# Attention in front of two feed-forward blocks on one core: row sums in 32-column products, transposes two pairs ahead

## The chip, the core and the metric

The kernel runs on one core of a Trainium2 chip. Its metric is the device time of one execution in microseconds. A core has five engines with queues of their own, each strictly in the order of the program: TensorE (PE: matmuls and transposes, fp32 results into PSUM), VectorE (DVE), ScalarE (ACT), GpSimd (POOL) and SyncE (SP, here for DMA issues alone). They meet through semaphores only: an instruction whose input or whose buffer is not ready holds up all that stands behind it on its engine. PSUM has eight banks of 128 partitions by 512 fp32.

## The reference

```python
def _attn_ref(q, k, v, cap):                      # 2 batches, 12 heads, 448 rows, 64 wide
    scores = np.matmul(q, k.transpose(0, 1, 3, 2)) / np.sqrt(64)
    scores = cap * np.tanh(scores / cap)
    scores = scores - np.max(scores, axis=-1, keepdims=True)
    attn = np.exp(scores)
    attn = attn / (np.sum(attn, axis=-1, keepdims=True) + 1e-09)
    return np.matmul(attn, v)
```

The heads side by side are the input (896 tokens by 768) of a feed-forward block (768 to 2048 to 768, with h * sigmoid(1.702 h)), whose output goes through a second one (RMS norm, a gate and a value of 1536, a projection to 768). All is fp32; the result must have nearly fp32 accuracy.

## The kernel before

**Numbers in two parts.** Most products are made of a high part in the type float32r and a rest: hi*hi + hi*lo + lo*hi, one pass of the array each. A product of plain fp32 operands (P*V, the row sums, transposes with the identity) needs no parts; the trace shows two passes for such a product. Weights are taken apart on the fly, unit by unit: `square`, `sign`, `mask` (ScalarE), `mid`, `top`, `low` (VectorE), `high_part` (ScalarE), `low_part` (VectorE), each on 128 x 768, each needing the one before. The first four units are decoded during attention: the list `early` (line 399) has 30 such steps, 15 for each of the two engines, and `decode(n)` emits the next n at its place in the loop. `low(w)` also issues the load of unit w + 3.

**Attention, pair by pair.** Two heads make a pair p (0 to 11); they lie side by side on the 128 partitions. For a pair
- `load_kq` and `load_v` bring k, q and v for a group of one to three pairs (`GROUPS`) over SyncE's queue, in chunks of 128 rows and a last one of 64;
- `turn(p)` transposes k and q on TensorE, eight 128 x 128 transposes into PSUM pool `ps_t` (one buffer);
- `split_kq(p)` makes the high parts and rests `x` on VectorE (two operations on 896 columns), and GpSimd copies the last 64 rows of k into a block-diagonal tile `kb`;
- `scores(p, c)` makes a strip of 128 key rows for c = 0, 1, 2, below also S(p,c): six passes on half the array's rows, two side by side, into pool `ps_s` (two buffers). `scores_last(p)` makes the last 64 rows of both heads in one strip of three full passes, into `ps_v` (two buffers);
- `exps(p, c)` is two operations on ScalarE: tanh, which frees the PSUM buffer, below tanh(p,c), and exp into tile `tt` (six buffers) or `tl`;
- `outputs(p)` is P*V, below P*V(p): six fp32 products on 64 columns of the array (tile position by head), then one on all 128 columns for the last strip, into `ps_v`; VectorE copies it to `z`;
- `add_two` (VectorE) and `add_third` (GpSimd) add the three wide strips of exponentials into `ts`; `sums(p)` multiplies `ts` by ones on 64 columns and the last strip by `blk` on 128, into `ps_v`;
- of pairs 0 to 8 the sums go by a short way: VectorE copies them to `sc`, GpSimd's DMAs fold one row of each head over 64 partitions (`rs`), `recips` (three iterations later) takes 7 reciprocals a partition and writes them to DRAM (`recs`), `spread` brings them back as a broadcast over 128 partitions (`r`, below r(p)). Pairs 9 to 11 take a reciprocal of 128 x 448 out of PSUM;
- `normal(p)` multiplies and takes the result apart into `xA` (VectorE: `norm_mul`, `norm_hi`, `norm_lo`; the copy of pairs 10 and 11 on ScalarE).

**The order.** Nothing is scheduled by a planner: the loop at line 420 emits the work of iteration p, and each engine executes its share in that order. A buffer is handed on in the order of allocation: with two buffers, the n-th tile of a pool waits for the last reader of tile n - 2. Iteration p is: S(p,1), exponentials of strips 0 and 1, `turn(p+1)`, `split_kq(p+1)`, `recips(p-3)`, `add_third(p-1)`, `spread(p-3)`, P*V(p-1), a decode step, S(p,2), S(p+1,0), the last strip, their exponentials, `normal(p-4)`, `add_two(p)`, two decode steps, `sums(p-1)`, loads. Iteration 12 holds what is left of pair 11, whose norm is emitted in the next stage.

**The next stage** (`rest`) runs the feed-forward blocks in one stream of matmuls (lines 521 to 523 and 724). It begins with three column blocks on the first 384 tokens (`HEAD`, 54 matmuls), then the same on the other 512, which need all twelve pairs.

Of the kernel before, what the change touches and what calls it, by code (L numbers as in the profile page):

```python
# [18 lines left out]
def attn_moe_kernel(  # L19
# [156 lines left out]
    def attention():  # L176
        with ExitStack() as actx:
# [12 lines left out]
            raws = [{nm: ap_.tile([128, NC + 1, 6 - 2 * i, D], F32, name=f"{nm}{i}", bufs=1) for nm in "kq"} for i in range(2)]  # L190


            vns = [ap_.tile([128, NC, 6 - 2 * i, D], F32, name=f"vn{i}", bufs=1) for i in range(2)]
            ves = [ap_.tile([128, 3 - i, 2, D], F32, name=f"ve{i}", bufs=1) for i in range(2)]
            kbs = [ap_.tile([128, 2, 128], F32R, name=f"kb{i}", bufs=1) for i in range(2)]

            def constants():
                for r in raws:
                    for nm in "kq":
                        nc.gpsimd.memset(r[nm][64:128, NC], 0.0)  # L200
# [9 lines left out]
            xs, pt, zt, nr, ts_ = {}, {}, {}, {}, {}  # L210

            def rows(src_, p0, n, c):

                b, h0 = divmod(2 * p0, H)
                return src_[b, h0:h0 + 2 * n, c * 128:min(c * 128 + 128, S)]

            def load_kq(g, nm, src_, eng=None):
                t, (p0, n) = raws[g % 2][nm], GROUPS[g]
                for c in (*range(NC), NC):
                    m = 128 if c < NC else 64  # L220
                    (eng or nc.sync).dma_start(out=t[0:m, c, 0:2 * n], in_=rows(src_, p0, n, c).rearrange("h p d -> p h d"))

            def load_v(g):
                p0, n = GROUPS[g]
                for c in range(NC):
                    nc.sync.dma_start(
                        out=vns[g % 2][:, c, 0:2 * n], in_=rows(v, p0, n, c).rearrange("h p d -> p h d")
                    )
                for e in range(2):
                    nc.sync.dma_start(  # L230
                        out=ves[g % 2][half[e], 0:n, e], in_=rows(v, p0, n, NC)[e:2 * n:2].rearrange("h p d -> p h d")
# [4 lines left out]
            def turn(p):  # L236

                g, i = place[p]
                if p:
                    t = ps_t.tile([128, 2, 512], F32, tag="t", name="t")  # L240
                    ts = [t[:, 0], t[:, 1]]
                else:

                    t = None
                    ts = [ps_t.tile([128, 2, 512], F32, tag="t", name="tk")[:, 0],
                          ps_s.tile([128, 2, 512], F32, tag="s", name="tq")[:, 0]]
                for j in (range(2) if p else (1, 0)):
                    r = raws[g % 2]["kq"[j]]
                    for c in range(NC + 1):
                        nc.tensor.transpose(  # L250
                            ts[j][:, c * 128:(c + 1) * 128], r[:, c, 2 * i:2 * i + 2].rearrange("p h d -> p (h d)"), ident
                        )
                turned[p] = t, ts

            def split_kq(p):
                t, ts = turned.pop(p)
                if p:
                    x = ap_.tile([128, 2, 2, S], F32R, tag="x", name="x")
                    xs[p] = [[x[:, a, j] for j in range(2)] for a in range(2)]
                    nc.vector.tensor_copy(x[:, 0], t[:, :, 0:S])  # L260
                    nc.vector.tensor_tensor(out=x[:, 1], in0=t[:, :, 0:S], in1=f(x[:, 0]), op=ALU.subtract)
                    for e in range(2):
                        nc.gpsimd.tensor_copy(kbs[p % 2][half[e], :, half[e]], f(x[half[e], :, 0, 384:S]))
                else:
                    xs[p] = [[ap_.tile([128, S], F32R, name=f"x{a}{j}", bufs=1) for j in range(2)] for a in range(2)]
                    for j in (1, 0):
                        nc.scalar.activation(out=xs[p][0][j], in_=ts[j][:, 0:S], func=AF.Copy)
                    for j in (1, 0):
                        nc.vector.tensor_tensor(out=xs[p][1][j], in0=ts[j][:, 0:S], in1=f(xs[p][0][j]), op=ALU.subtract)
# [27 lines left out]
            def exps(p, c, ps):  # L297
# [3 lines left out]
                else:  # L301
                    t = ap_.tile([128, 2, S], F32, tag="tt", name="tt", bufs=6)
# [5 lines left out]
            def outputs(p):  # L308
# [3 lines left out]
                for c in range(NC):  # L312
# [5 lines left out]
                nc.tensor.matmul(  # L318
                    out=ps[:, 0:S], lhsT=ves[g % 2][:, i].rearrange("p h d -> p (h d)"), rhs=pt[p, NC],
                    start=False, stop=True, skip_group_check=True,  # L320
                )
# [6 lines left out]
            def add_two(p):  # L328
                ts_[p] = ap_.tile([128, 2, S], F32, tag="ts", name="ts")
                nc.vector.tensor_tensor(out=ts_[p], in0=pt[p, 0], in1=pt[p, 1], op=ALU.add)  # L330

            def add_third(p):
                nc.gpsimd.tensor_tensor(out=ts_[p], in0=ts_[p], in1=pt[p, 2], op=ALU.add)  # L333

            def sums(p):

                ps = ps_v.tile([128, 512], F32, tag="v", name="v")
                streams = [ts_[p]] if p < NPR - 1 else [pt[p, c] for c in range(NC)]
                for n, t in enumerate(streams):
                    for e in range(2):  # L340
                        nc.tensor.matmul(  # L341
                            out=ps[half[e], 0:S], lhsT=f(ones)[:, half[e]], rhs=t[:, e],
                            start=(n == 0), stop=False, skip_group_check=True,
                        )
                nc.tensor.matmul(  # L345
                    out=ps[:, 0:S], lhsT=blk, rhs=pt[p, NC], start=False, stop=True, skip_group_check=True
                )
                if p < NPR - 3:
                    sc = zrp.tile([128, S], F32, tag="sc", name="sc", bufs=2)
                    nc.vector.tensor_copy(sc, ps[:, 0:S])  # L350
                    nr[p] = zrp.tile([128, S // 64], F32, tag="rs", name="rs", bufs=3)
                    for e in range(2):
                        nc.gpsimd.dma_start(
                            out=nr[p][half[e]], in_=sc[64 * e:64 * e + 1, :].rearrange("o (a n) -> o a n", a=64)
                        )
                else:
# [3 lines left out]
            def recips(p):  # L360
                rs = nr[p]
                nc.vector.reciprocal(out=rs, in_=rs)
                nr[p] = dram.tile([2, S], F32, tag="recs", name="recs")
                nc.gpsimd.dma_start(out=nr[p].rearrange("e s -> (e s)").rearrange("(p n) -> p n", p=128), in_=rs)
# [21 lines left out]
            load_kq(0, "q", q, nc.scalar)  # L386
            load_kq(0, "k", k)
# [3 lines left out]
            load_kq(1, "k", k)  # L391
            load_kq(1, "q", q)
# [437 lines left out]
```

## Time and profile before

| | us |
|---|---|
| median of three runs | 633.44 (632.35 to 634.41) |
| the profiled execution | 634.12 |
| span of its profile, first to last instruction | 632.3 |
| TensorE busy in the span | 616.2 (97%) |
| VectorE, ScalarE, GpSimd busy | 462.2, 399.2, 99.5 |

In the profile, PE is a matmul pass or transpose and PEld a weight load; L314 is line 314. A matmul's end is modelled and runs past the start of the next one, so the time that a block of matmuls takes is read from its start to the next block's start.

### The profile page before, as it was taken

How to read it: one execution, taken by the hardware profiler on the slowest of the kernel's cores; microseconds unless marked ns; L12 is line 12 of the kernel's file. 1: busy time of each engine (PE TensorE's matmuls, PEld its weight loads, DVE VectorE, ACT ScalarE, POOL GpSimd, SP SyncE). 2: the span in 40 equal slices, each digit the busy share in tenths (PEclk: the TensorE clock that was granted, in tenths of full speed). 3: DMA queues.
4: the chain of work that ended last, by engine and by line, in shares of the span. 5: the costliest groups of instructions: out<-in, count | busy, mean ns of one | idle time of the engine just before them, and what ended most of it. 6: DMA issues, size and time to landing. Idle time of an engine off the chain costs nothing.

```text
span 632.3 us, 8124 instructions
## 1 busy us (share of the span) xinstructions
PE 616.2 (97%) x3126; PEld 511.0 (81%) x3126; DVE 462.2 (73%) x555; ACT 399.2 (63%) x533; POOL 99.5 (16%) x122
## 2 busy tenths in 40 slices
PE   7999898899999999999999999999999999999997
PEld 4544444368889889988889989999988899999997
DVE  3467989896867463667678889998378887688842
ACT  5779977819978464777766765667355675355500
POOL 3245454500000000000002211210022200022100
PEclk9899999999999999999999999999999999999999
DMA  6854523222444333233333333335232234232012
GB/s 140 193 145 113 123 61 97 78 66 74 140 138 137 112 101 100 83 117 102 106 133 104 109 100 102 101 107 173 71 99 101 100 111 140 78 122 101 0 68 107
DMA packets 85445, 67.16 MB, mean 106 GB/s; under 512 B 39444, under 2 KB 82726, under 8 KB 85408
## 3 DMA queue, kind: packets, MB, share of 16 engines
q1 hardware_dynamic: 80240, 64.27, 33.4%
q0 software_dynamic: 4208, 2.16, 1.3%
q8 instruction: 24, 0.39, 0.3%
q10 hardware_dynamic: 960, 0.23, 0.2%
q14 instruction: 13, 0.11, 0.1%
HBM read 63.80 MB, written 2.78 MB: 105 GB/s over the span
## 4 chain that ended last, share of the span: by engine, by line
PE 86%; DVE 4%; DMA 3%; POOL 3%; issue 3%; SPq 1%; POOLq 0%
PE b L523 21%; PE b L522 21%; PE b L521 21%; PE b L724 14%; PE v L314 2%; POOL ts L333 2%; PE s L282 1%; PE v L341 1%; DMA r<-recs 1%; PE t L250 1%; PE v L345 1%; DMA recs<-rs 1%; DVE x L260 1%; DMA q<-in_q 1%; PE v L318 1%
## 5 line engine op out<-in xcount | busy, mean ns | idle before, releaser
L523 PE MATMUL b<-x,ring 128*128 128x512 f32 (+1 forms) x480 | 174.2, 363 | 0.0
L521 PE MATMUL b<-x,ring 128*128 128x512 f32 (+1 forms) x480 | 174.1, 363 | 0.0
L522 PE MATMUL b<-x,ring 128*128 128x512 f32 (+1 forms) x480 | 174.0, 363 | 0.0
L522 PEld LDWEIGHTS b<-x,ring 128*128 128x128 f32 x480 | 90.1, 188 | 10.0 <-issue 0.2
L521 PEld LDWEIGHTS b<-x,ring 128*128 128x128 f32 x480 | 90.1, 188 | 10.0 <-issue 0.2
L523 PEld LDWEIGHTS b<-x,ring 128*128 128x128 f32 x480 | 90.1, 188 | 9.4
L136 DVE SCALAR_TENSOR_TENSOR dec<-raw,dec 128x768 uint32<-128x768 uint32 x68 | 71.5, 1052 | 26.6 <-ACT dec L132 25.4
L724 PE MATMUL b<-ring,uA 128*128 128x384 f32 x504 | 87.8, 334 | 0.0
L724 PEld LDWEIGHTS b<-ring,uA 128*128 128x128 f32 x504 | 87.4, 188 | 0.0
L142 DVE SCALAR_TENSOR_TENSOR dec<-raw,dec 128x768 uint32<-128x768 uint32 x68 | 74.9, 1102 | 1.1
L162 DVE TENSOR_TENSOR ring<-dec,ring 128x768 fp32r<-128x768 f32 x68 | 68.5, 1008 | 3.6 <-ACT ring L157 3.6
L523 PE MATMUL b<-g,ring 128*128 128x384 f32 (+1 forms) x192 | 70.0, 365 | 0.0
L522 PE MATMUL b<-g,ring 128*128 128x384 f32 (+1 forms) x192 | 69.8, 364 | 0.0
L521 PE MATMUL b<-g,ring 128*128 128x384 f32 (+1 forms) x192 | 69.6, 362 | 0.0
L157 ACT ACTIVATE ring<-dec 128x768 fp32r<-128x768 f32 x68 | 56.7, 833 | 19.0 <-DVE dec L148 10.7
L148 DVE SCALAR_TENSOR_TENSOR dec<-raw,dec 128x768 uint32<-128x768 uint32 x68 | 64.9, 955 | 1.4
L128 ACT ACTIVATE dec<-dec,edge 128x768 f32<-128x768 f32 x68 | 63.4, 932 | 0.9
L124 ACT ACTIVATE dec<-raw 128x768 f32<-128x768 f32 x68 | 60.9, 895 | 0.6 <-DVE ring L162 0.5
L692 POOL TENSOR_TENSOR a<-a,gg 128x512 f32<-128x512 f32 (+1 forms) x18 | 29.6, 1645 | 188.6 <-DVE gg L685 188.6
L132 ACT ACTIVATE dec<-dec 128x768 f32<-128x768 f32 x68 | 57.3, 842 | 1.5
L616 POOL TENSOR_TENSOR sqs<-sqs,sq 128x384 f32<-128x384 f32 (+1 forms) x10 | 11.7, 1172 | 231.8 <-ACT sq L612 231.8
L304 ACT ACTIVATE tt<-s,tsc 128x896 f32<-128x896 f32 x36 | 35.9, 996 | 16.5 <-PE s L282 15.6
(102 smaller groups left out, 715.1 us busy)
## 6 DMA issues: line engine op xcount, KB each, us to landing
raw<-in_moe_w_out SPq DMA_DIRECT2D x20, 768.0 KB, 4.2
raw<-in_moe_w_in SPq DMA_DIRECT2D x16, 768.0 KB, 4.7
raw<-in_moe_w_gate SPq DMA_DIRECT2D x12, 768.0 KB, 4.3
raw<-in_moe_w_val SPq DMA_DIRECT2D x12, 768.0 KB, 4.2
raw<-in_moe_w_out SPq DMA_DIRECT2D x8, 512.0 KB, 4.1
out<-oacc SPq DMA_DIRECT2D x6, 384.0 KB, 2.3
raw<-in_moe_w_out SPq DMA_DIRECT2D x8, 256.0 KB, 3.6
r<-recs POOLq DMA_DIRECT2D x9, 224.0 KB, 7.8
```

Of the source, the lines that this page charges most:

```text
L124: nc.scalar.activation(out=f(d), in_=f(r[:, :, 1]), func=AF.Square, scale=2.0 ** 15)
L128: nc.scalar.activation(out=f(d), in_=f(d), func=AF.Sign, bias=edge)
L132: nc.scalar.activation(out=f(d), in_=f(d), func=AF.Relu, scale=2.0 - 2.0 ** -23)
L136: nc.vector.scalar_tensor_tensor(out=d, in0=hi, scalar=3, in1=d, op0=ALU.logical_shift_left, op1=ALU.bitwise_and)
L142: nc.vector.scalar_tensor_tensor(out=d, in0=hi, scalar=0xC0000000, in1=d, op0=ALU.bitwise_and, op1=ALU.bitwise_or)
L148: nc.vector.scalar_tensor_tensor(out=d, in0=lo, scalar=29, in1=d, op0=ALU.logical_shift_right, op1=ALU.bitwise_or)
L157: nc.scalar.activation(out=t[:, 0], in_=f(dec_t[w][0]), func=AF.Copy)
L162: nc.vector.tensor_tensor(out=t[:, 1], in0=f(d), in1=f(t[:, 0]), op=ALU.subtract)
L521: nc.tensor.matmul(out=wide(o, b), lhsT=w0, rhs=x0, start=first, stop=False)
L522: nc.tensor.matmul(out=wide(o, b), lhsT=w0, rhs=x1, start=False, stop=False)
L523: nc.tensor.matmul(out=wide(o, b), lhsT=w1, rhs=x0, start=False, stop=last)
L724: nc.tensor.matmul(out=os_[t][n][:, 0:HW], lhsT=uA[xi][:, i, tok], rhs=w[:, wi, n * HW:(n + 1) * HW], start=(i == 0 and xi == 0 and wi == ...
```

## The change

- Row sums of pairs 0 to 8: `add_two`, `add_third` and `ts` go. The seven streams of exponentials are multiplied on tiles of 32 columns, four tiles a round and two rounds: strips 0 and 1 of both heads, then strip 2 and the last one. A head's sum is then in two rows, which four DMAs (instead of two) bring over, and `recips` adds them before the reciprocal. Pairs 9 to 11 multiply the three strips on 64 columns, and the last strip in two such products.
- P*V: the product of the last strip is two 64-column products instead of a full one.
- Transposes: k and q share a tile of seven chunks, in which the last 64 rows of k and the first 64 of q are one chunk; seven transposes make 896 contiguous columns. `turn` and `split_kq` run two pairs ahead.
- The loop: iteration p is now exponentials of strips 0 and 1, S(p,2), S(p+1,0), a decode step, exponentials of strip 2, the last strip, `turn(p+2)`, `split_kq(p+2)`, its exponentials, `recips(p-3)` and `spread(p-3)`, P*V(p-1), S(p+1,1), `normal(p-4)` (in iterations 11 and 12 also `normal(p-2)`), decode steps (two, in iterations 10 and 11 three and four), `sums(p-1)`, loads. `tt` has eight buffers.
- Loads: seven groups of one or two pairs, in another order of issue.
- In the next stage a tuple of functions is written in another way.

```diff
-            GROUPS = [(0, 1), (1, 2), (3, 3), (6, 2), (8, 2), (10, 2)]
+            GROUPS = [(0, 1), (1, 2), (3, 1), (4, 2), (6, 2), (8, 2), (10, 2)]
...
+                def flip(out, c):
+                    nc.tensor.transpose(out, raws[g % 2][:, c, 2 * i:2 * i + 2].rearrange("p h d -> p (h d)"), ident)
...
+                    t = ps_t.tile([128, 2, 512], F32, tag="t", name="t").rearrange("p a s -> p (a s)")
+                    for c in range(2 * NC + 1):
+                        flip(t[:, c * 128:(c + 1) * 128], c)
...
-                nc.tensor.matmul(
-                    out=ps[:, 0:S], lhsT=ves[g % 2][:, i].rearrange("p h d -> p (h d)"), rhs=pt[p, NC],
-                    start=False, stop=True, skip_group_check=True,
-                )
+                for e in range(2):
+                    nc.tensor.matmul(
+                        out=ps[half[e], 0:S], lhsT=ves[g % 2][:, i, e], rhs=pt[p, NC],
+                        start=False, stop=True, skip_group_check=True,
+                    )
...
+                if p < NPR - 3:
+                    for n in range(2):
+                        for e in range(2):
+                            for j in range(2):
+                                if n and j:
+                                    w, t = blk[:, 64 * e:64 * e + 32], pt[p, NC]
+                                else:
+                                    w, t = f(ones)[:, 0:32], pt[p, j + 2 * n][:, e]
+                                r0 = 64 * e + 32 * j
+                                nc.tensor.matmul(
+                                    out=ps[r0:r0 + 32, 0:S], lhsT=w, rhs=t,
+                                    start=(n == 0), stop=(n == 1), skip_group_check=True,
+                                )
...
             def recips(p):
                 rs = nr[p]
-                nc.vector.reciprocal(out=rs, in_=rs)
+                nc.vector.tensor_tensor(out=rs[:, 0], in0=rs[:, 0], in1=rs[:, 1], op=ALU.add)
+                nc.vector.reciprocal(out=rs[:, 0], in_=rs[:, 0])
...
-            s0 = scores(0, 0)
+            s0, s1 = scores(0, 0), scores(0, 1)
             for p in range(NPR + 1):
                 if p < NPR:
-                    ps = [s0, scores(p, 1)]
-                    for c in range(2):
-                        exps(p, c, ps[c])
-                if p + 1 < NPR:
-                    turn(p + 1)
-                    split_kq(p + 1)
+                    exps(p, 0, s0)
+                    exps(p, 1, s1)
+                    s2 = scores(p, 2)
+                    if p == 0:
+                        last = scores_last(p)
+                        turn(1)
+                        split_kq(1)
+                    if p + 1 < NPR:
+                        s0 = scores(p + 1, 0)
+                    if p > 2:
+                        decode(1)
+                    exps(p, 2, s2)
+                    if p:
+                        last = scores_last(p)
+                    if p + 2 < NPR:
+                        turn(p + 2)
+                        split_kq(p + 2)
+                    exps(p, NC, last)
                 if 3 <= p < NPR:
                     recips(p - 3)
-                if 1 <= p < NPR:
-                    add_third(p - 1)
-                if 3 <= p < NPR:
                     spread(p - 3)
                 if p >= 1:
                     outputs(p - 1)
...
+                if p + 1 < NPR:
+                    s1 = scores(p + 1, 1)
                 if p >= 4:
                     normal(p - 4)
-                if p < NPR - 1:
-                    add_two(p)
-                if p >= 1:
-                    decode(2 if p > 2 else 0)
-                    sums(p - 1)
                 if p >= NPR - 1:
                     normal(p - 2)
...
+                if 2 < p < NPR:
+                    decode((2, 3, 4)[max(0, p - NPR + 3)])
+                if p >= 1:
+                    sums(p - 1)
+
+                for g, at_ in ((2, 0), (3, 0), (4, 1), (5, 3), (6, 5)):
+                    if p == at_:
+                        load_k(g)
+                        load_q(g)
+                if p in (1, 3, 4, 6, 8):
+                    load_v(2 + (1, 3, 4, 6, 8).index(p))
```

## Rows read from the trace of the kernel before

**Rows 1.** Windows: stretch, length, busy (count) of PE PEld DVE ACT POOL, clock, DMA.

```profile
12.94:19.77 6.83, 6.54 (x25) 3.76 (x26) 3.13 (x3) 4.06 (x5) 1.38 (x2) 0.50 0.92 209
19.77:134.25 114.48, 106.34 (x545) 48.68 (x544) 91.69 (x102) 89.78 (x104) 51.22 (x67) 1.00 0.42 105
134.25:632.30 498.05, 494.43 (x2526) 452.94 (x2524) 365.16 (x444) 299.02 (x418) 41.34 (x28) 1.00 0.32 104
```

**Rows 2.** Timeline of PE, one pass of the loop: start, length, instruction, count.

```profile
29.67 2.48 PE L314 MATMUL v<-tt,vn 128*64 128x448 f32 x12
...
33.02 1.50 PE L282 MATMUL s<-x 64*128 64x448 f32 x12
34.46 0.88 PE L292 MATMUL v<-x,kb 128*128 128x448 f32 x3
35.26 0.97 PE L341 MATMUL v<-ts,ones 128*64 128x448 f32 x4
36.16 1.02 PE L345 MATMUL v<-tl,blk 128*128 128x448 f32 x2
37.12 0.87 PE L282 MATMUL s<-x 64*128 64x448 f32 x6
37.92 0.66 PE L250 MATMUL t<-ident,k 128*128 128x128 f32 x4
...
38.94 0.97 PE L314 MATMUL v<-tt,vn 128*64 128x448 f32 x4
```

**Rows 3.** Waits before 134.25: who, for whom, us in total, times, longest.

```profile
PE v L341 <- POOL ts L333: 8.1, 9, 2.0
```

**Rows 4.** Groups by line and form, 0 to 190: busy, mean ns, idle before.

```profile
L333 POOL TENSOR_TENSOR ts<-ts,tt 128x896 f32<-128x896 f32 x11 | 23.7, 2157 | 0.7
L330 DVE TENSOR_TENSOR ts<-tt 128x896 f32<-128x896 f32 x11 | 16.0, 1453 | 0.0
L353 POOL DMA_DIRECT2D rs<-sc x18 | 9.5, 534 | 21.7 <-DVE sc L350 21.7
L362 DVE RECIPROCAL rs<-rs 128x7 f32<-128x7 f32 x9 | 1.7, 185 | 0.0
```

**Rows 5.** Line 314, 29.6 to 29.9: min/median/max ns, first and last start.

```profile
L314 PE MATMUL v<-tt,vn x2: 590/590/590, 29.7 to 29.7; 128*64 128x448 f32 x2
```

**Rows 6.** Timeline of ACT, iterations 8 and 10 (columns as in rows 2).

```profile
99.76 0.84 ACT L157 ACTIVATE ring<-dec 128x768 fp32r<-128x768 f32 x1 [3.76 <-DVE dec L148]
...
115.94 0.61 ACT L304 ACTIVATE tl<-v,tsc 128x448 f32<-128x448 f32 x1
...
117.16 0.92 ACT L128 ACTIVATE dec<-dec,edge 128x768 f32<-128x768 f32 x1
117.99 0.99 ACT L304 ACTIVATE tt<-s,tsc 128x896 f32<-128x896 f32 x1
...
119.96 0.99 ACT L304 ACTIVATE tt<-s,tsc 128x896 f32<-128x896 f32 x1
```

**Rows 7.** Timeline of SP, the issues of q for pairs 3 to 5.

```profile
16.89 2.29 SPq L221 DMA_DIRECT2D q<-in_q  x3
```

**Rows 8.** Chain that ended last, 71 to 87: start, length, what.

```profile
78.69 7.81 DMA r<-recs
```

**Rows 9.** Timeline of POOL, iterations 6 and 7 (columns as in rows 2).

```profile
81.87 0.58 POOL L364 DMA_DIRECT2D recs<-rs  x1
...
87.39 0.83 POOL L369 DMA_DIRECT2D r<-recs  x1 [2.77 <-DMA recs<-rs]
```

**Rows 10.** Timeline of DVE, the end of attention (columns as in rows 2).

```profile
128.33 2.95 DVE L358 RECIPROCAL r<-v 128x448 f32<-128x448 f32 x1
131.20 0.56 DVE L372 TENSOR_TENSOR r<-z,r 128x448 f32<-128x448 f32 x1
...
132.77 0.95 DVE L136 SCALAR_TENSOR_TENSOR dec<-raw,dec 128x768 uint32<-128x768 uint32 x1
```

**Rows 11.** Line 369, all of it: its time from issue to landing.

```profile
DMA to landing us min/median/max: 6.7/7.8/9.1
```

More of the change, by code (lines that the diff above doesn't have):

```diff
@@ L226, in load_v @@
                     nc.sync.dma_start(
-                        out=vns[g % 2][:, c, 0:2 * n], in_=rows(v, p0, n, c).rearrange("h p d -> p h d")
+                        out=vns[g % 2][:, c, 0:2 * n], in_=rows(v, p0, n, c * 128, c * 128 + 128)
                     )
@@ L230, in load_v @@
                     nc.sync.dma_start(
-                        out=ves[g % 2][half[e], 0:n, e], in_=rows(v, p0, n, NC)[e:2 * n:2].rearrange("h p d -> p h d")
+                        out=ves[g % 2][half[e], 0:n, e], in_=rows(v, p0, n, NC * 128, S)[:, e:2 * n:2]
                     )
@@ L255, in split_kq @@
+                turned[p] = t
             def split_kq(p):
-                t, ts = turned.pop(p)
+                t = turned.pop(p)
                 if p:
[L258 to L261, printed above, removed]
+                    x = ap_.tile([128, 2, 2 * S], F32R, tag="x", name="x")
+                    xs[p] = [[x[:, a, j * S:(j + 1) * S] for j in range(2)] for a in range(2)]
+                    nc.vector.tensor_copy(x[:, 0], t[:, 0:2 * S])
+                    nc.vector.tensor_tensor(out=x[:, 1], in0=t[:, 0:2 * S], in1=f(x[:, 0]), op=ALU.subtract)
@@ L326, in outputs @@
                     nc.scalar.activation(out=zt[p], in_=ps[:, 0:S], func=AF.Copy)
[L328 to L333, printed above, removed]
             def sums(p):
                 ps = ps_v.tile([128, 512], F32, tag="v", name="v")
-                streams = [ts_[p]] if p < NPR - 1 else [pt[p, c] for c in range(NC)]
-                for n, t in enumerate(streams):
+                if p < NPR - 3:
+                    for n in range(2):
+                        for e in range(2):
+                            for j in range(2):
+                                if n and j:
[6 more added lines that the diff above has]
+                                    start=(n == 0), stop=(n == 1), skip_group_check=True,
+                                )
+                    sc = zrp.tile([128, S], F32, tag="sc", name="sc", bufs=2)
+                    nc.vector.tensor_copy(sc, ps[:, 0:S])
+                    nr[p] = zrp.tile([128, 2, S // 64], F32, tag="rs", name="rs", bufs=3)
+                    for e in range(2):
+                        for j in range(2):
+                            r0 = 64 * e + 32 * j
+                            nc.gpsimd.dma_start(
+                                out=nr[p][half[e], j], in_=sc[r0:r0 + 1, :].rearrange("o (a n) -> o a n", a=64)
+                            )
+                else:
+                    for c in range(NC):
+                        for e in range(2):
+                            nc.tensor.matmul(
+                                out=ps[half[e], 0:S], lhsT=f(ones)[:, half[e]], rhs=pt[p, c][:, e],
+                                start=(c == 0), stop=False, skip_group_check=True,
+                            )
@@ L340, in sums @@
                     for e in range(2):
                         nc.tensor.matmul(
-                            out=ps[half[e], 0:S], lhsT=f(ones)[:, half[e]], rhs=t[:, e],
-                            start=(n == 0), stop=False, skip_group_check=True,
-                        )
[L345 to L356, printed above, removed]
+                            out=ps[half[e], 0:S], lhsT=blk[:, half[e]], rhs=pt[p, NC],
@@ L390, in attention @@
             load_v(0)
[L391 to L392 removed]
+            load_k(1)
+            load_q(1)
             load_v(1)
```

81 lines of the change are left out of this document (33 added, 48 removed).

## The prediction

> **What bounds the kernel now.** I read the busy times by stage first [rows 1]. From 134.25 us to the end TensorE is busy for 494.4 of 498.05 us at the full clock. The change reaches into that stage only with one rewritten tuple, so it keeps its length. What can move is attention, the first 134.25 us.
>
> The matmul timeline gives one undisturbed pass of the pair loop [rows 2]. From the starts of its blocks: P*V of twelve 64-column passes and a full-width one 3.35 us, two score strips 1.44, the last strip 0.80, row sums 0.90 + 0.96, a score strip 0.80, eight transposes 1.02. Together 9.27. Twelve pairs at that rate would be 111 us. Attention is longer, because later row sums wait for the addition on GpSimd: 8.1 us in nine waits [rows 3]. So attention is bound by TensorE, then by that addition, which itself waits for VectorE.
>
> **The change: what TensorE executes.** Two 64-column passes side by side, one step, cost (2.48 - 0.97) / 4 = 0.378 us inside a run (twelve passes against four), and the next block starts some 0.07 before a run's printed end [rows 2]. P*V as one run of 16 passes is 0.97 + 6 x 0.378 - 0.07 = 3.17 instead of 3.35. Seven transposes instead of eight: 1.02 - 0.11 = 0.91. The scores and the last strip cost what they did; shared tiles only reorder them.
>
> The trace has no 32-column product. Row sums of one pair are now 16 passes. If four tiles run at once, that is 4 steps: 0.97 + 2 x 0.378 - 0.07 = 1.65. If only two do, 8 steps: 3.17. Gain beyond four is excluded, since there are four tiles. The nearest row is a pair of 64-column tiles: in this stretch of 0.3 us two passes of 590 ns both start at 29.7 [rows 5], and no third one does. As a product's own two passes share a tile and can't overlap, the second tile's first pass has overtaken the first tile's second one. Each tile then has its own queue, and I take 1.65, keeping 3.17 for the range. The Trainium skill ("TensorE: Matmul & The Clock Gate", Part 3: Packing small matmuls) says instead that matmuls start and end strictly in program order; by that rule two-pass products on four tiles would keep only two of them busy and the sums would cost the upper price. The 64-column starts speak against the rule, and no run here shows four tiles.
>
> The new block sum is 3.17 + 1.44 + 0.80 + 1.65 + 0.80 + 0.91 = 8.77. Last strip and transposes are now neighbours of one shape, which may save part of a change of shape (a full-width product occupies 0.96, two bare steps 0.76 [rows 2]); I take 8.7. For pairs 9 and 10 the sums get dearer, 3.17 instead of 1.86, because `ts` is gone.
>
> **What other engines execute.** Eleven additions go from VectorE (1.45 each) and from GpSimd (2.16) [rows 4]. Added: a tiny addition before each small reciprocal, an estimated 0.2 by that reciprocal (0.185), and two DMA issues of 0.53 a pair on GpSimd in place of the 2.16 [rows 4]; both queues have room. `spread` now stands right behind `recips`, so GpSimd waits there for `recs` to land; behind it are the four issues of the next sums and the copies into `kb`, which are needed only two last strips later: nothing on the path. The bank of P*V(p) is now that of sums(p-1), emptied on VectorE behind normal(p-4). By the steps below that copy ends about 2 us into the next iteration, P*V starts at 3.15: covered by 1 us, and if a broadcast is later than that, TensorE waits. ScalarE needs 3 x 1.97 for a pair's wide strips (117.99 to 119.96), 1.22 for the last, and 15 decode steps of 0.83 over nine iterations: 8.5 an iteration [rows 6]. It is just below TensorE's 8.7, so any wait on ScalarE now reaches TensorE.
>
> **The loads.** Seven groups instead of six are 13 more issues on SyncE, at about 0.6 each some 8 us of a queue with nothing but loads, while the bytes stay. In the order of the queue each group still lands an iteration or more before its transposes or P*V, pair 3's q excepted (next part), and the first weights land near 37, when square(0) comes up. I cost them at nothing; a late group would cost TensorE its lateness. Four memsets less at the start lie beside the loads.
>
> **The start.** The second pair's loads arrive as before. Pair 3's q is issued until about 18.2 [rows 7]; with some 2.9 to landing turn(3) starts near 21.1 (other waits, on tanh(1,1), end at 19.4). Then 0.91 + 3.17 + 0.80 + 1.65: iteration 2 starts at 27.6. Six iterations of 8.7 bring iteration 8 to 79.8.
>
> **Iterations 8 and 9: a queue wait.** Here high_part(1) stands on ScalarE ahead of pair 9's exponentials. It needs low(1), which stands on VectorE behind the copy of P*V(7) and normal(4). It costs the old kernel 3.76 on ScalarE, at no loss to TensorE [rows 6]; there the score strips came later. From iteration 8's start: P*V(7) ends at 6.3, its copy (0.6, as other operations on 448 columns) at 6.9; normal(4) needs the broadcast r(4). That takes 7.8 us, and a `recs` issued while the previous broadcast is in flight is awaited until it has landed (issued 81.87, next broadcast at 87.39, the previous landed at 86.50) [rows 8, 9]. So broadcasts follow each other at 7.8 + 0.9 = 8.7, the iteration's own pace, and in the steady state each lands about 7.4 into an iteration. From there: normal 1.6 [rows 10], low(1) 0.9, high_part(1) 0.85, tanh(9,0) 1.0: 11.8 instead of 8.7. S(9,2) needs that tile: 3.0 idle. S(10,0) needs tanh(9,1), 2.0 later, and S(9,2) fills only 0.7: 1.3 idle. Iteration 9 lasts 13.0; iteration 10 starts at 79.8 + 8.7 + 13.0 = 101.5.
>
> **The last three iterations.** From there, without transposes: sums(9) end at 9.4. VectorE: copy 6.0, normal(6) from 7.4 (its broadcast) to 9.0, low(2) 9.9, the wide reciprocal of pair 9 to 12.8 (2.95 [rows 10]). ScalarE: high_part(2) 10.8, tanh(11,0) 11.8. So S(11,2) starts at 11.8, not 9.4 (2.4 idle); last strip to 13.4; P*V(10) to 16.6. sums(10) needs the bank of the last strip: exp(11,0), strip 1, mask(3), strip 2 and its tanh end at 18.2 (1.65 idle); sums(10) to 21.4, P*V(11) to 24.6. sums(11) needs sums(10)'s bank, which reciprocal(10) reads. Ahead of that on VectorE: copy to 17.2, normal(7) and normal(9) 3.2, four decode steps 3.6, the reciprocal 2.95: 27.0 (2.35 idle). sums(11) end at 30.1. The next stage begins with 54 products on columns that pair 11 doesn't fill, some 9 to 10 us (0.197 each as a mean of both widths [rows 1]); pair 11's reciprocal and norm take about 5: covered. If that cover went, each us late would cost one.
>
> **The sum.** The second stage starts at 101.5 + 30.1 = 131.6 instead of 134.25: 2.65 us gained. The profiled execution took 634.12 (span 632.3 plus 1.8 around it), 0.68 above the median of the three runs, so it would become 631.5, and the median 633.44 becomes 630.8. The removed waits and additions would be worth some 13 us; about 10.7 us of new idle time behind ScalarE and VectorE give most of it back.
>
> **Rivals.**
> Two tiles at a time: the nine 32-column sums cost 1.52 more. Iteration 2 starts at 29.1, iterations last 10.2, iteration 8 starts at 90.3. The waits partly vanish in the longer iterations (2.4 left in iteration 9, the broadcast in time at the end): 90.3 + 10.2 + 12.6 + 29.0 = 142.1, so 641.3, slower. It decides from 0.3 us more per sum. For it: nothing in the trace reads four streams at once. Against: the overtaking in [rows 5]. Chance 0.15. The Trainium skill's rule of program order, weighed above, would end here.
> The new waits are covered: if broadcasts come earlier and VectorE's chain shortens, the 10.7 us shrink. With none the stage starts at 120.9 and the time is 620.1, with half 625.4. For it: no idle time of TensorE in the old trace has this cause. Against: the queue orders are fixed in the code, and the durations are measured. Chance 0.20.
> Dearer waits: a broadcast of 9.1 instead of the median 7.8 [rows 11] adds 1.3 at iterations 8 and 10, 633.4. Or the clock: it stood at half (1.2 GHz) from 12.94 to 19.77, after TensorE had waited for its loads [rows 1]; idle stretches of 3.0 and 2.4 are longer than the old loop's longest on the additions (2.0 [rows 3]), and 6.8 us at half rate cost up to 3.4: 634.2. Together 0.18.
>
> **How the numbers follow.** My forecast, 630.8, holds 0.47 with 628 to 634 as its own range. About 0.3% (1.9 us) can be told from no change. Faster than 631.5: 0.28 of the forecast's share and the 0.20 of covered waits, 0.48. Within: 0.33. Slower: two tiles 0.15 and a rest of dear waits, 0.19. The range 622 to 637 leaves out the two-tile case and the lowest of the covered one.
>
> **What would show it.** The timeline of matmuls: sums blocks of 1.65 with four starts within some 20 ns, or 3.17 with two; iterations 3 to 8 of 8.7; P*V blocks of 3.17. On ScalarE a wait of about 5 us before high_part(1), on TensorE idle time before S(9,2) put down to tanh, before S(11,2), and before sums(11) put down to the reciprocal. GpSimd without additions. Wrong would be: a second stage that changes its length, iterations well off 8.7 before iteration 8, or TensorE waiting for loads.

## The result: slower, and the profile after

| | before | after |
|---|---|---|
| median | 633.17 us (four runs beside the changed kernel) | 641.16 (638.68 to 642.66) |
| ratio to before | | 1.0121 [1.0083, 1.0158] |
| the profiled execution | 634.12 | 638.68 |
| its span | 632.3 | 636.9 |

The forecast was 630.8 with a range of 622 to 637. The time lies outside it, on the other side of no change. Run again beside the last experiments, the changed kernel took 640.20, 1.0117 [1.0095, 1.0139].

The stages of the changed kernel, as windows that begin where iterations 2, 8, 9, 10 and the second stage begin (columns as in [rows 1]):

```profile
27.92:82.99 55.07, 52.44 (x364) 25.69 (x361) 30.69 (x48) 49.76 (x58) 21.90 (x45) 1.00 0.59 148
82.99:97.82 14.83, 8.72 (x64) 4.32 (x61) 9.95 (x16) 6.18 (x9) 5.83 (x11) 0.97 0.14 30
97.82:109.51 11.69, 11.21 (x60) 5.93 (x61) 4.69 (x9) 10.40 (x12) 2.66 (x7) 0.75 0.46 123
109.51:137.14 27.63, 23.64 (x131) 9.44 (x127) 19.89 (x28) 13.75 (x17) 5.19 (x9) 1.00 0.28 81
```

TensorE's share of work went down as planned. What replaced it is idle time: 6.1 us in iteration 8 alone. Against the steps of the forecast:

| stage | forecast | measured | late by |
|---|---|---|---|
| start, to iteration 2 | 27.6 | 27.92 | 0.3 |
| iterations 2 to 7 | 52.2 | 55.07 | 2.9 |
| iteration 8 and the wait behind it | 11.7 | 14.83 | 3.1 |
| iteration 9 | 10.0 | 11.69 | 1.7 |
| iterations 10 to 12 | 30.1 | 27.63 | -2.5 |
| second stage | 498.05 | 499.8 (137.14 to 636.9) | 1.7 |

Together 7.2 us, which is 638.7 instead of 631.5 for the profiled execution. It is the fastest of its four. The profile of the second set is of its slowest execution (643.44): it shows the same waits, a longer one in the second stage (3.50 instead of 1.96, see below), and TensorE's clock at half in three more stretches than the one in iteration 9 that is shown below (granted 0.50 in 16.82 to 20.23, 122.63 to 126.04 and 146.52 to 149.94).

**The blocks on TensorE are what was forecast.** Matmul timeline, iterations 7 and 8 (columns as in [rows 2]; line 347 is the 32-column sums, 320 and 325 P*V):

```profile
71.21 1.31 PE L347 MATMUL v<-tt,ones 128*32 128x448 f32 x9
...
72.85 0.86 PE L288 MATMUL s<-x 64*128 64x448 f32 x6
74.44 0.87 PE L288 MATMUL s<-x 64*128 64x448 f32 x6 [0.73 <-ACT tt L310]
...
77.39 2.48 PE L320 MATMUL v<-tt,vn 128*64 128x448 f32 x12 [0.51 <-DVE sc L352]
79.69 0.92 PE L325 MATMUL v<-tl,ve 128*64 128x448 f32 x4
80.55 0.87 PE L288 MATMUL s<-x 64*128 64x448 f32 x6
```

Sums take 72.85 - 71.21 = 1.64 us, P*V 80.55 - 77.39 = 3.16. Line 347 in the stretch 71.20 to 71.24:

```profile
L347 PE MATMUL v<-tt,ones x4: 563/563/563, 71.2 to 71.2; 128*32 128x448 f32 x4
```

Four passes of 563 ns start within 0.04 us: four tiles work at once. (A product is two passes; the sums of a pair are 8 products, so 16 passes.)

**The waits do not come from there.** Waits up to 140 us (columns as in [rows 3]):

```profile
POOL r L387 <- DMA recs<-rs: 33.5, 9, 5.0
...
ACT ring L157 <- DVE dec L148: 16.0, 3, 8.6
DVE r L390 <- DMA r<-recs: 13.4, 6, 3.0
...
PE s L288 <- ACT tt L310: 8.8, 5, 5.0
...
PE v L320 <- DVE sc L352: 3.0, 4, 1.1
```

Read from below: P*V waits for the copy of the sums (3.0 us), strips for tanh (8.8 in five waits, the longest 4.96). Behind the P*V waits and the longest tanh wait is VectorE waiting for broadcasts (13.4), and behind that GpSimd, which cannot issue the next broadcast until `recs` has landed (33.5). The chain of waits shows the longest case link by link, 83 to 98 us:

```profile
81.08 4.82 DMA recs<-rs
85.90 0.28 issue
86.18 7.21 DMA r<-recs
93.39 0.02 issue
93.41 0.64 DVE r L390
...
95.04 0.96 DVE dec L148
96.01 0.02 issue
96.03 0.84 ACT ring L157
96.87 0.91 ACT tt L310
```

A broadcast lands at 93.39; normal(4), low(1), high_part(1) and tanh(9,0) follow one another. TensorE, same stretch:

```profile
97.82 1.49 PE L288 MATMUL s<-x 64*128 64x448 f32 x6 [4.96 <-ACT tt L310]
99.79 1.49 PE L288 MATMUL s<-x 64*128 64x448 f32 x6 [0.48 <-ACT tt L310]
...
103.91 0.97 PE L320 MATMUL v<-tt,vn 128*64 128x448 f32 x4
```

After 4.96 us idle six passes take 1.49 instead of 0.87. The granted clock of 97.82 to 109.51 is 0.75 in the window above: half of full rate (1.2 instead of 2.4 GHz) for the first blocks, until P*V at 103.91 is quick again. From the first of these strips to P*V it is 6.09 us. The same blocks at full clock, in the run with the normalisations last (below), take 4.34, though the second strip waits longer there:

```profile
89.27 0.89 PE L288 MATMUL s<-x 64*128 64x448 f32 x6 [0.94 <-ACT tt L310]
91.24 0.87 PE L288 MATMUL s<-x 64*128 64x448 f32 x6 [1.09 <-ACT tt L310]
...
93.61 2.48 PE L320 MATMUL v<-tt,vn 128*64 128x448 f32 x12
```

So the clock cost 6.09 - 4.34 = 1.8 us. Iterations 2 and 3 took 8.6; of the 3.1 that iteration 9 takes beyond that, the other 1.3 are the second strip's wait for tanh, of which only 0.48 shows as idle time because the strip before it runs slowly.

The second stage waits 1.96 us for a bank that reciprocal(11) still reads. PE, then VectorE:

```profile
133.98 2.48 PE L363 MATMUL v<-tt,ones 128*64 128x448 f32 x12 [0.64 <-ACT z L333]
...
142.49 0.44 PE L541 MATMUL b<-x,ring 128*128 128x384 f32 x1 [1.96 <-DVE r L373]
```

```profile
139.49 2.95 DVE L373 RECIPROCAL r<-v 128x448 f32<-128x448 f32 x1
```

### The profile page after: what moved, and what is told of

Its sections match the earlier page's. It is cut to its first block, busy times and chain, and to the rows that moved or that the text cites. A ratio compares the mean times of both kernels' runs of the same rounds, so it can differ in the third digit from the quotient of the medians.

```text
span 636.9 us, 8389 instructions
## 1 busy us (share of the span) xinstructions
PE 612.9 (96%) x3251; PEld 511.6 (80%) x3251; DVE 437.8 (69%) x553; ACT 399.8 (63%) x533; POOL 82.8 (13%) x125
## 4 chain that ended last, share of the span: by engine, by line
PE 82%; DMA 8%; DVE 4%; ACT 3%; SPq 2%; issue 1%; POOL 0%; ACTq 0%; DVEq 0%; POOLq 0%
PE b L543 21%; PE b L542 21%; PE b L541 21%; PE b L744 14%; DMA r<-recs 4%; DMA recs<-rs 2%; PE v L320 2%; ACT tt L310 1%; PE s L288 1%; DMA kq<-in_q 1%; DVE r L373 1%; SPq L218 1%; DMA kq<-in_k 1%; DMA raw<-in_moe_w_in 1%; PE v L298 1%
## 5 line engine op out<-in xcount | busy, mean ns | idle before, releaser
L136 DVE SCALAR_TENSOR_TENSOR dec<-raw,dec 128x768 uint32<-128x768 uint32 x68 | 69.7, 1025 | 26.7 <-ACT dec L132 25.3
L142 DVE SCALAR_TENSOR_TENSOR dec<-raw,dec 128x768 uint32<-128x768 uint32 x68 | 73.2, 1076 | 1.1
L162 DVE TENSOR_TENSOR ring<-dec,ring 128x768 fp32r<-128x768 f32 x68 | 66.8, 984 | 3.6 <-ACT ring L157 3.6
L148 DVE SCALAR_TENSOR_TENSOR dec<-raw,dec 128x768 uint32<-128x768 uint32 x68 | 64.9, 955 | 1.4
L715 ACT ACTIVATE uA<-a 128x512 fp32r<-128x512 f32 (+1 forms) x24 | 13.9, 578 | 46.4 <-POOL a L712 34.5
L636 POOL TENSOR_TENSOR sqs<-sqs,sq 128x384 f32<-128x384 f32 (+1 forms) x10 | 11.7, 1169 | 236.0 <-ACT sq L632 236.0
```

The source lines that it names most:

```text
L136: nc.vector.scalar_tensor_tensor(out=d, in0=hi, scalar=3, in1=d, op0=ALU.logical_shift_left, op1=ALU.bitwise_and)
L142: nc.vector.scalar_tensor_tensor(out=d, in0=hi, scalar=0xC0000000, in1=d, op0=ALU.bitwise_and, op1=ALU.bitwise_or)
L148: nc.vector.scalar_tensor_tensor(out=d, in0=lo, scalar=29, in1=d, op0=ALU.logical_shift_right, op1=ALU.bitwise_or)
L162: nc.vector.tensor_tensor(out=t[:, 1], in0=f(d), in1=f(t[:, 0]), op=ALU.subtract)
```

## The experiments

Two theories. A: late broadcasts reach TensorE through what stands behind a normalisation on VectorE, and the longest wait also lowers the clock. B: the new TensorE blocks themselves cost the time. The chip's runs of the kernel before gave 633.68 to 633.75 beside these.

### The sums alone, in the old loop

```diff
 (the kernel before)
-  add_two(p) ... add_third(p - 1) ... streams = [ts_[p]]
+  sums, rs and recips as in the changed kernel; tt has eight buffers
```

> The kernel before with nothing but the new row sums: 32-column products for pairs 0 to 8, four rs DMAs, the small addition, no ts additions on VectorE and GpSimd, sums of pairs 9 to 11 from their strips, eight tt tiles. Transposes, strips, P*V and their order stay. Theory A: the waits on GpSimd's addition go (8.1 us), sums cost 1.65 instead of 1.86, and the old place of the strips covers a late high_part(1); the chain of broadcasts at 9.9 a pair keeps the iterations from falling below it, so 626 to 633, faster than before. Theory B (the new sums cost the time): slower than before, 636 or more.

629.78 us, 0.9934 [0.9912, 0.9956]: faster than before. All that TensorE waits for on other work of the loop:

```profile
PE s L282 <- ACT tt L304: 1.3, 2, 1.1
...
PE v L356 <- DVE r L366: 1.0, 1, 1.0
PE b L528 <- DVE r L366: 0.9, 1, 0.9
```

The 8.1 us of [rows 3] are gone, and iterations take 74.77 - 65.70 = 9.07 (starts of P*V), though broadcasts are issued 8.4 to 11.0 apart here too. Theory B falls for the sums: they are the good part. No pass waits for the copy of the sums. In this order P*V(p-1), the last strip and the sums take the two banks in turn, so P*V inherits the last strip's, which ScalarE empties. That this is the reason is argued from the order, not tried by itself.

### The sums and P*V, in the old loop

```diff
 (the run above)
-  nc.tensor.matmul(out=ps[:, 0:S], lhsT=ves[...].rearrange(...), rhs=pt[p, NC], ...)
+  for e in range(2):
+      nc.tensor.matmul(out=ps[half[e], 0:S], lhsT=ves[g % 2][:, i, e], rhs=pt[p, NC], ...)
```

> The kernel before with the new row sums (as the run with the old loop and new sums, 629.8) and with the last piece of P*V as two 64-column products, so that P*V is one run of column tiles. Order, transposes and strips stay old. P*V goes from 3.35 to 3.17 in eleven pairs: 2.0 less, 627.8, if TensorE paces that loop. If the chain of broadcasts paces it (9.7 between issues there too), the 2 us turn into waits and the time stays at 629.5 to 630.

631.74, 0.9969 [0.9959, 0.998]: neither of the two times expected; not faster than without the edit, rather slower. The early iterations do shrink to 8.87, but strips then wait for VectorE and ScalarE, and this stands at the end:

```profile
127.66 3.84 PE L357 MATMUL v<-tt,ones 128*64 128x448 f32 x12 [2.11 <-DVE r L367]
131.29 1.30 PE L362 MATMUL v<-tl,blk 128*64 128x448 f32 x4
```

Twelve passes take 3.84 instead of 2.48 after an idle time of 2.11; the granted clock of 127.66 to 132.51 is 0.65. In this profile TensorE's saving turned into waits and a slower clock.

### No broadcast

```diff
-  nc.gpsimd.dma_start(out=nr[p], in_=d.unsqueeze(1).to_broadcast([2, 64, S]))
...
-  nc.vector.tensor_tensor(out=nr[p], in0=zt.pop(p), in1=nr[p], op=ALU.mult)
+  nc.vector.tensor_tensor(out=nr[p], in0=zt.pop(p), in1=nr[p] if p >= NPR - 3 else unit, op=ALU.mult)
...
   (unit: a tile of ones, filled once)
```

> The changed kernel without the broadcast DMA of the reciprocals; the normalisation of pairs 0 to 8 multiplies by a tile of ones instead, so their division is left out. All other steps and DMAs stay. Theory A (the broadcast chain, 9.9 us a pair, is what the loop keeps to, and what makes high_part(1) late): iterations 4 to 8 take 8.6 to 8.7 us instead of 8.5 to 10.1, P*V waits for the copy of the sums no more (3.0 us before), the idle time of 4.96 us shrinks to under 2 and the clock stays up: 630 to 634. Theory B (the new TensorE blocks cost the time): within 1 us of the changed kernel.

634.64, 0.9998 [0.9975, 1.0021], some 6 us less than the changed kernel and just above the range expected. Iterations take 8.6; P*V no longer waits for the sums' copy. What is left in the main:

```profile
PE s L288 <- ACT tt L310: 4.5, 4, 2.6
PE b L542 <- DVE r L373: 2.4, 1, 2.4
```

The 2.6 is the chain low(1), high_part(1), tanh(9,0) without a wait for a broadcast: a price of the order itself, and near the 3.0 that I had forecast. After these 2.57 us the clock fell too (six passes in 1.28, then 1.49), which had not been expected.

### high_part one place later

```diff
-  + [(high_part, 1), (mid, 2), (square, 3), ...
+  + [(mid, 2), (high_part, 1), (square, 3), ...
...
-  + [(high_part, 2), (mask, 3), (low_part, 2), ...
+  + [(mask, 3), (high_part, 2), (low_part, 2), ...
```

> The changed kernel with two neighbours swapped in the list of early decode steps, twice: (mid, 2) ahead of (high_part, 1), and (mask, 3) ahead of (high_part, 2). high_part(1) then stands on ScalarE behind the first two exponentials of pair 9, no longer ahead of them. Theory A (the late broadcast reaches TensorE through high_part(1), and the idle time lets the clock fall): the idle time before the third strip of pair 9 falls from 4.96 us to under 1.5, the clock stays at full rate after 97 us, and the time falls by 4 to 7 us, to 634 to 637; not the whole 4.96 + 3, since P*V(8) then waits some 1.8 us for the copy of the sums, behind normal(4). Theory B (the new TensorE blocks themselves cost the time): no change, 641.

639.97, 1.0098 [1.0069, 1.0127]: a miss. The idle time of 4.96 is gone as expected, and the clock of 96 to 104 us is full. But TensorE now waits elsewhere:

```profile
PE v L320 <- DVE sc L352: 5.8, 5, 1.7
PE b L541 <- DVE r L373: 4.0, 1, 4.0
PE v L320 <- DVE rs L377: 3.1, 1, 3.1
```

The last broadcast is issued at 126.38 instead of 127.43. The chain came 1 us earlier; work that runs ahead of it waits at the next place that needs it (the 3.1 are one wait, of P*V(10), behind the wide reciprocal of pair 9). The clock fell after the wait of 4.04 in the second stage (granted 0.59 in 140 to 147). So mending this one place brought nothing by itself.

### Fewer small DMAs

```diff
-  for j in range(2):
+  for j in range(1):
...
-  nc.vector.tensor_tensor(out=rs[:, 0], in0=rs[:, 0], in1=rs[:, 1], op=ALU.add)
```

> The changed kernel with two of the four rs DMAs of each pair, as many as the kernel before has; the half sums of the other two tiles and their addition are left out. Theory A (the four rs land one by one, 0.2 us each, behind the broadcast, and the next broadcast has to wait for them and recs: that is why the chain takes 10.0 a pair instead of the 8.7 that I had read): the time from a broadcast's landing to the next issue falls from a mean of 1.75 us (2.0, 1.2, 1.6, 2.2) to 1.2 to 1.4, the chain to 9.5, P*V's waits from 3.0 to 1.5 us, the idle time before the third strip of pair 9 to 3 to 4, and the time by 1 to 3 us. Rival (the small DMAs don't matter; the broadcasts themselves take longer, or TensorE's own order paces the chain): the turn stays at 1.6 or more and the time within 1 us of the changed kernel.

641.33, 1.0136 [1.0112, 1.0161]: as the changed kernel, so the rival's time. The turn from a landing to the next issue is 0.8 at two places (1.2 and 1.4 in the changed kernel) and 2.3, 1.7 and 1.8 at three, almost as there (2.0, 1.6, 2.2). At two of these three (the 2.3 and the 1.8) `recs` lands behind loads of q and v that SyncE issued during the broadcast. In the changed kernel, line 231 (v) in 44 to 46 us, with no broadcast under way at their issue, and in 77 to 82, with one:

```profile
DMA to landing us min/median/max: 3.3/3.4/3.5
...
DMA to landing us min/median/max: 7.4/7.8/8.1
```

So four small DMAs instead of two are not what makes the chain long. By the landings it is the broadcast and the loads that land right behind it; no run took the loads away.

### The small DMAs on another queue

```diff
-  nc.gpsimd.dma_start(out=nr[p][half[e], j], in_=sc[r0:r0 + 1, :]...)
+  nc.sync.dma_start(out=nr[p][half[e], j], in_=sc[r0:r0 + 1, :]...)
   (and recs likewise)
```

> The changed kernel with the four rs DMAs and the recs DMA of each pair issued by SyncE instead of GpSimd, so that they no longer stand in one queue behind the broadcast. Theory A, first form (the four rs and the recs land only after the broadcast because they share its queue; that makes 9.9 of 8.2): broadcasts follow each other at the pace of the iterations, 8.6 to 9.0, the 3.0 us of P*V waits fall under 1, the idle time before the third strip of pair 9 falls to about 3, as I had forecast for a chain of 8.7; 633 to 638. Second form (the broadcast occupies all DMA engines, whatever the queue): rs still land just after the broadcast, and the time stays at 640 to 642.

652.14, 1.0284 [1.0241, 1.0327]. Line 357, `rs` on SyncE's queue, issued in 29 to 33 and in 52 to 54.5 us:

```profile
DMA to landing us min/median/max: 1.8/1.9/1.9
...
DMA to landing us min/median/max: 3.6/4.3/4.9
```

The second four were issued 2.7 us into a broadcast and landed right after it, on another queue than its own. So here a second queue did not get past a broadcast (second form). The reason that I gave for that form, all DMA engines occupied, is not what the trace shows. While a broadcast of the changed kernel ran almost alone, the 16 engines were busy 14% in the mean, about as much as two of them (columns as in [rows 1], DMA share next to last):

```profile
86.30:93.30 7.00, 5.67 (x38) 1.96 (x38) 3.82 (x7) 1.15 (x2) 3.89 (x8) 1.00 0.14 35
```

Why other DMAs still land behind it is open. The run is 11 to 12 us slower than the changed kernel besides: SyncE's waits for `sc` now hold up the loads behind them, so its time says nothing on theory A.

### The chain one iteration earlier

```diff
-  if 3 <= p < NPR:
-      recips(p - 3); spread(p - 3)
+  if 2 <= p < NPR - 1:
+      recips(p - 2); spread(p - 2)
```

> The changed kernel with the reciprocals and the broadcast of a pair started one iteration earlier (pair p-2 instead of p-3 in iteration p); the normalisations stay where they are. The pace of the chain (about 9.9 a pair) is untouched, it only starts some 9 us ahead. Theory A (P*V waits and the larger part of the 4.96 us are lateness of that chain): the P*V waits for the copy of the sums (3.0 us) vanish, the idle time before the third strip of pair 9 falls to the 2.6 us that the kernel without broadcasts has, and the time to that kernel's: 633 to 636. Rival (the chain paces the loop whenever it starts, since each broadcast is held up by the four small DMAs of its own iteration): P*V still waits over 2 us in all, and 639 or more.

656.74, 1.0359 [1.0342, 1.0377]: a clear miss, and the rival's direction. Waits on VectorE:

```profile
DVE rs L377 <- DMA rs<-sc: 43.8, 8, 8.8
```

The `rs` of pair p-2 are issued behind the broadcast of pair p-3 and land after it. Asked for one iteration later they hold VectorE, and the copies that free TensorE's banks stand behind that. The third iteration of lag was what kept `rs` off VectorE's path.

### The second stage's wait

```diff
 (in the order in which the last round emits them)
-  normal(8); normal(10); sums(11)
+  sums(11); normal(8); normal(10)
```

> The changed kernel with one move in the last round of the pair loop: the row sums of pair 11 and their reciprocal come ahead of the normalisations of pairs 8 and 10. Theory A (the second stage's second column block waits 1.96 us because its bank is still read by reciprocal(11), which stands on VectorE behind two normalisations and the last broadcast): reciprocal(11) ends some 3 us behind the sums, the wait falls under 0.3, and the time by about 2, to 639. Rival (the second stage then waits for the normalised columns instead): as long as the changed kernel, 641.

637.62, 1.0062 [1.0044, 1.008]. TensorE's wait in the second stage (on line 541, here 543) is gone. The gain of 2.6 to 3.5 on the two medians of the changed kernel is more than the 1.96 of its first profile; in the profile of its second set of runs that wait was 3.50.

### The normalisations last

```diff
-  normal(p - 4) ... normal(p - 2)
   decode(...); sums(p - 1)
+  normal(p - 4) ... normal(p - 2)
...
-  r: bufs=3
+  r: bufs=5
```

> The changed kernel with the normalisations moved behind the row sums in each round, so that on VectorE the copy of the sums and the decode step low come ahead of the wait for the broadcast; the r tiles grow from three to five, which that order needs. The broadcasts, their DMAs and every TensorE block stay. Theory A (the broadcast reaches TensorE only through what stands behind the normalisation on VectorE: the copy that frees the bank of P*V, low(1) ahead of high_part(1), reciprocal(11)): P*V waits and the wait of the second stage vanish, the idle time before the third strip of pair 9 falls under 1.5, the clock stays up there, second stage from 125 to 129, 623 to 630: faster than the kernel before. Rival (the loop is held by the chain of DMAs or by the new TensorE blocks themselves): 636 or more.

625.94 (624.5 to 631.02), 0.9894 [0.9851, 0.9937]: faster than both kernels. TensorE's waits:

```profile
PE s L288 <- ACT tt L310: 2.8, 3, 1.1
...
PE v L320 <- DVE r L373: 1.5, 1, 1.5
...
PE b L541 <- DVE r L373: 0.2, 1, 0.2
```

None is for the copy of the sums. The second stage starts at 124.72 instead of 137.14, and in this profile, of the fastest of the four executions, the granted clock is 1.00 from 20 us to the end (0.989 in the mean in the one of 631.02). Every broadcast, DMA and TensorE block is still there; what changed is what stands behind the normalisations on VectorE, and the number of `r` tiles, for which nothing waited before: all nine waits ahead of the broadcasts' issues are for `recs`. So theory B falls for the other TensorE blocks too, and the path of theory A is shown. Its word "late" covers only part of the gain: this run is also 8.7 us faster than the one without any broadcast (634.64). Some 6 us are the broadcasts' lateness. The rest, as far as these two runs tell them apart, is the normalisation's own work ahead of low(1) and reciprocal(11) (waits of 2.57 and 2.38 in that run), with the clock that fell there.

### Both edits

```diff
 (the run above)
-  (high_part, 1), (mid, 2) ... (high_part, 2), (mask, 3)
+  (mid, 2), (high_part, 1) ... (mask, 3), (high_part, 2)
```

> Two edits of earlier runs together on the changed kernel: normalisations behind the row sums (625.9 alone), and high_part(1) and high_part(2) one place later on ScalarE's list (640.0 alone). With the normalisations last, the idle time left in the pair loop is 0.94 and 1.09 before strips of pair 9, behind high_part(1), and 1.45 before P*V(10). The order takes the first two away and adds none if the broadcasts reach TensorE no more: 1 to 2 us less, 624 to 625, and the clock full throughout. Rival (what is gained there turns up again at P*V(10) or at the second stage): 626.

622.37 (622.08 to 623.28), 0.9827 [0.9814, 0.984]: the best version, 18 us under the changed kernel and 11 under the kernel before. The second stage starts at 122.46:

```profile
20.00:122.46 102.46, 100.31 (x661) 47.71 (x661) 65.81 (x98) 87.45 (x102) 37.81 (x74) 1.00 0.52 130
```

The order that brought nothing certain by itself brings 3.6 on the medians here, more than the 1 to 2 expected; between executions at full clock (624.50 there, 622.08 to 623.28 here) it is 1.2 to 2.4. Both idle times before strips of pair 9 are gone; in the second stage a wait of 1.2 us stands where it was 0.2.

The changed kernel itself was the eleventh run:

> The changed kernel once more, on the chip of these runs, so that the edits can be compared with it in one place: 639 to 643 as before, with 4 to 5 us of idle time before the third strip of pair 9 and one stretch at half clock behind it.

640.20, as expected: 4.72 us idle before the third strip of pair 9, which then takes 1.49. Not one stretch at half clock, though, but the four named above.

## Why the prediction was wrong, step by step

- **Sums 1.65, P*V 3.17: right** (1.64, 3.16). The overtaking in [rows 5] was the right row to lean on. The Trainium skill ("TensorE: Matmul & The Clock Gate", Part 3: Packing small matmuls) lets matmuls start and end strictly in program order. I had read that for single passes, and so read it does not hold: the first passes of four products start within 0.04 us, before the second pass of any (these start from 71.61). The products did start in the order of the program; the rule read for whole products is not refuted here.
- **Start 27.6: right in number (27.92), partly by luck.** Pair 3's q landed at 20.72, as forecast (21.1), but TensorE came to turn(3) only at 21.47, from a wait for tanh that ended at 19.94 instead of 19.4. In the second profile, with half clock before that, P*V(0) starts at 23.86 instead of 22.32.
- **The broadcast chain at 8.7, each landing 7.4 into an iteration: the step that failed.** I added the median 7.8 of [rows 11] to one turn, from a landing to the next issue, 0.9 [rows 9]. The eight turns of the old trace are 0.7 to 6.2, so one of them was no measure. Measured, the four periods from 46 to 86 us are 10.3, 8.9, 10.6 and 10.4, mean 10.05: 8.3, 7.8, 9.0, 8.2 from issue to landing and turns of 2.0, 1.2, 1.6, 2.2. With 8.7 the chain kept TensorE's own pace; with 10.05 the iterations stretched to 8.9 to 10.1. The start of the chain was wrong as well: the first broadcast, with none before it, landed 9.2 into iteration 4, the next four 10.0, 11.1, 11.2 and 10.4 into theirs. For r(4) that is 3.0 later than my 7.4, and S(9,2) came 3.0 later into iteration 8 (14.83 instead of 11.8): 1.8 from the first landing, 1.2 from the slower chain. Issue times on GpSimd:

```profile
45.98 0.83 POOL L387 DMA_DIRECT2D r<-recs  x1 [2.75 <-DMA recs<-rs]
...
56.29 0.82 POOL L387 DMA_DIRECT2D r<-recs  x1 [4.11 <-DMA recs<-rs]
...
65.22 0.83 POOL L387 DMA_DIRECT2D r<-recs  x1 [3.51 <-DMA recs<-rs]
...
75.81 0.82 POOL L387 DMA_DIRECT2D r<-recs  x1 [5.03 <-DMA recs<-rs]
...
86.18 0.83 POOL L387 DMA_DIRECT2D r<-recs  x1 [4.55 <-DMA recs<-rs]
```

  In the two longest turns (2.0 and 2.2) loads of v land between the broadcast and `recs`. The chain is not the whole miss: without any broadcast the time is 634.64, still 3.8 above the forecast.
- **"Covered by 1 us": fell with it.** The copy that frees P*V's bank stands behind normal(p-4). I had seen it and named the condition ("if a broadcast is later than that, TensorE waits"), then priced it at nothing. It cost 3.0 us in iterations 5 to 8.
- **The queue wait at high_part(1): right in kind, too small.** 4.96 instead of 3.0; the 1.3 behind it came as forecast (0.48 of it as idle time). Without broadcasts it is 2.6 + 0.7, so the forecast was nearly the price of the order alone.
- **The clock: named as a rival, too cheap a chance.** It fell in iteration 9 and cost 1.8 us (I had 3.4 at most). I gave "dearer waits" 0.18 with broadcast and clock apart; both came. The broadcasts of the four periods took 8.3 instead of 7.8 in the mean, and with the long idle time gone (high_part one place later) the clock stayed full at that place.
- **The last three iterations: 27.63 instead of 30.1.** Idle 1.92 before S(11,2) and 1.43 before sums(10) (forecast 2.4 and 1.65), but 0.64 before sums(11) instead of 2.35: it took the bank of P*V(11), which ScalarE empties. My rule "the n-th tile waits for tile n - 2" is not how that bank was handed on.
- **"The second stage keeps its length": wrong by 1.7**, the other side of the same bank: sums(11) now lie in one that the second stage's second column block takes, and reciprocal(11) reads it late.
- **Rivals.** Two tiles at a time: refuted by four starts at once, although its 641.3 is, by coincidence, what came out. Covered waits: no, but with the normalisations last the second stage starts at 124.7, as between none and half of the waits.

Still open: why single broadcasts take 6.8 to 9.0 us. In the changed kernel's first profile the five with a load issued in their first 2 us took 8.2 to 9.0 and the other four 6.8 to 7.8, but no run took the loads away. Nor did a run spread the broadcast, which alone kept the DMA engines 14% busy, over more of them.

## What to carry to other kernels

A part that is faster by itself (the sums: 629.8) can make a kernel slower when its neighbours move a wait under TensorE's path: list for each PSUM bank which instruction frees it and what stands ahead of that on its queue. Put an operation that waits for a long DMA last on its engine in each round, so that copies that free banks go first; here that was 14 to 15 us, the clock included. A chain of DMAs is to be timed with the loads that will run beside it, from its first link on, and not by one row.

## What the runs showed of the hardware

- Fp32 products on four tiles of 32 columns run side by side: 8 products (16 passes) of 448 columns in 1.64 us, four passes starting within 0.04 us; the 8 products of P*V on two tiles of 64 columns take 3.16.
- Small DMAs and loads issued more than 1.1 us into a broadcast DMA of 224 KB (6.8 to 9.0 us in the changed kernel) landed behind it in every profile here, on its own and on another engine's queue: 1.9 became 4.3 us, 3.4 became 7.8. That is so although one that ran almost alone kept the 16 DMA engines only 14% busy. Some issued sooner landed during it (q, issued 0.24 us into one: 2.6 us).
- In the changed kernel, idle times of 4.96 and 4.72 us in mid-kernel were followed by half clock; in its first profile 1.92 and 1.96 were not, in the second 2.03 was (six passes in 1.37). The ten executions of this one program took 638.66 to 643.44 us, at mean granted clocks from 0.995 down to 0.986.
